# Attention and a SoLU feed-forward in one kernel: where the exponentials are added up, when a transpose is issued, and in which PSUM banks outputs lie

## The chip, the cores and the metric

The kernel runs on one core of a Trainium2 chip. The time is that of the device, in microseconds (us), as the median of several runs; lower is better. A profile of one execution shows every instruction of the core's engines: TensorE (PE, with its weight loads as PEld), VectorE (DVE), ScalarE (ACT), GpSimd (POOL) and SyncE (SP), which issues most of the transfers.

## The reference

Two blocks are joined. The first is attention with normalised queries and keys, for 8 batches of 12 heads with 448 tokens and 64 columns. Its result, as 3584 rows of 768, goes through a feed-forward with a softmax-weighted unit and a layer norm.

```python
def _attn_ref(q, k, v, g_q, g_k):                     # q, k, v: (8, 12, 448, 64) float32
    def rmsnorm(x, g):
        rms = np.sqrt(np.mean(x * x, axis=-1, keepdims=True) + 1e-06)
        return x / rms * g
    q_n, k_n = (rmsnorm(q, g_q), rmsnorm(k, g_k))
    scores = 1.0 / np.sqrt(q.shape[-1]) * np.matmul(q_n, k_n.transpose(0, 1, 3, 2))
    scores = scores - np.max(scores, axis=-1, keepdims=True)
    attn = np.exp(scores)
    attn = attn / (np.sum(attn, axis=-1, keepdims=True) + 1e-09)
    return np.matmul(attn, v)

def _moe_ref(x, w_in, w_out, g_ln):                   # x: (3584, 768), w_in: (768, 1024), w_out: (1024, 768)
    h = x @ w_in
    e = np.exp(h - np.max(h, axis=-1, keepdims=True))
    solu = h * (e / (np.sum(e, axis=-1, keepdims=True) + 1e-09))
    mu = np.mean(solu, axis=-1, keepdims=True)
    var = np.mean((solu - mu) ** 2, axis=-1, keepdims=True)
    return ((solu - mu) / np.sqrt(var + 1e-06) * g_ln) @ w_out

# reference: x = attn_out.transpose(0, 2, 1, 3).reshape(B * S, H * D); return _moe_ref(x, ...)
```

The weights arrive as 64-bit floats; the kernel converts them to 32 bits on the chip.

## The kernel before

The kernel takes two heads at a time, a "pair" (48 of them). `h0` is on partitions 0 to 63 and `h1` on 64 to 127 of the tiles that have the head's columns on the partitions. Scores are computed with the keys on the partitions, in four pieces `kc` of 112 keys, and their exponentials E are used as they are: the values are summed over keys by TensorE, the sum of the exponentials too, by a matmul with ones, and the division comes last. PSUM has eight banks of 512 float32 a partition: tile `h` takes two, the two buffers of tag "t" two banks each, the two buffers of tag "o" one each.

```python
    loads = ctx.enter_context(tc.tile_pool(name="loads", bufs=2))
    work = ctx.enter_context(tc.tile_pool(name="work", bufs=2))
    small = ctx.enter_context(tc.tile_pool(name="small", bufs=4))
    ps_h = ctx.enter_context(tc.tile_pool(name="ps_h", bufs=1, space=bass.MemoryType.PSUM))
    ps_t = ctx.enter_context(tc.tile_pool(name="ps_t", bufs=2, space=bass.MemoryType.PSUM))
    # ...
    def normalise(n):
        d = st[n]
        d["qkn"] = work.tile([P, 2 * NB, 32], FP32, tag="qkn", name="qkn", bufs=1)
        nc.gpsimd.tensor_tensor(
            d["qkn"],
            d["qk"].rearrange("p s b d -> p (s b) d"),
            d["y"].rearrange("p b -> p b ()").to_broadcast([P, 2 * NB, 32]),
            OP.mult,
        )

    def qk_transpose(n):
        d = st[n]
        d["qkT"] = work.tile([P, 2, S], FP32, tag="qkT", name="qkT")
        nc.vector.transpose(d["qkT"].rearrange("p s t -> p (s t)"), d["qkn"].rearrange("p b d -> p (b d)"))

    def gain(n):
        d = st[n]
        nc.scalar.activation(d["qkT"][:, 0], d["qkT"][:, 0], AF.Copy, scale=gcol[:, KF : KF + 1])

    def fold_sums(n):
        d = st[n]
        nc.vector.tensor_tensor(d["ss"], d["ss"], d["part"], OP.add)

    def scores(n, kc):
        d = st[n]
        if kc == 0:
            d["E"] = work.tile([SP, NJ, 2, S], FP32, tag="E", name="E")
        s = ps_t.tile([SP, 2, 512], FP32, tag="t", name="s")
        for h in range(2):
            hh = slice(h * D, (h + 1) * D)
            nc.tensor.matmul(
                s[:, h, 0:S], d["qkT"][hh, 1, kc * SP : (kc + 1) * SP], d["qkT"][hh, 0, :], start=True, stop=True
            )
        nc.scalar.activation(d["E"][:, kc], s[:, :, 0:S], AF.Exp)

    def add(n, kc):
        d = st[n]
        if kc == 1:
            d["es"] = work.tile([SP, 2, S], FP32, tag="es", name="es")
            nc.gpsimd.tensor_tensor(d["es"], d["E"][:, 0], d["E"][:, 1], OP.add)
        else:
            nc.vector.tensor_tensor(d["es"], d["es"], d["E"][:, kc], OP.add)

    def values(n):
        d = st[n]
        d["o"] = ps_t.tile([P, S], FP32, tag="o", name="o")
        for kc in range(NJ):
            for h in range(2):
                nc.tensor.matmul(
                    d["o"][h * D : (h + 1) * D, :], d["v"][:, h, kc], d["E"][:, kc, h],
                    start=(kc == 0), stop=(kc == NJ - 1),
                )

    def sums(n):
        d = st[n]
        d["sm"] = ps_t.tile([P, S], FP32, tag="o", name="sm")
        for h in range(2):
            nc.tensor.matmul(
                d["sm"][h * D : (h + 1) * D, :], ones[0:SP, :], d["es"][:, h], start=True, stop=True
            )

    def divide(n):
        b, hp = divmod(n, NP)
        d = st[n]
        if b // 2 not in xTs:
            xTs[b // 2] = work.tile([P, KD, 2 * S], FP32, tag="xT", name="xT")
        r = work.tile([P, NB, 32], FP32, tag="r", name="r", bufs=1)
        rc = small.tile([P, NB], FP32, tag="rc", name="rc")
        nc.vector.transpose(r.rearrange("p b i -> p (b i)"), d["sm"])
        nc.vector.reciprocal(rc, r[:, :, 0])
        nc.vector.transpose(r, rc.rearrange("p b -> p b ()").to_broadcast([P, NB, 32]))
        c0 = (b % 2) * S
        nc.vector.tensor_tensor(xTs[b // 2][:, hp, c0 : c0 + S], d["o"], r.rearrange("d b i -> d (b i)"), OP.mult)
        del st[n]
```

The feed-forward works on tiles of 128 rows: two halves of h, a softmax and a layer norm (`ff_max`, `ff_moments`, `ff_norm`, issued one, two and three units later), the transpose of u, and two halves of the output.

```python
    def ff_in(t, half):
        m, i = divmod(t, 2 * S // P)
        d = mt.setdefault(t, {})
        if half == 0:
            d["h"] = ps_h.tile([P, DFF], FP32, tag="h", name="h")
        hs = slice(half * 512, half * 512 + 512)
        for c in range(KD):
            nc.tensor.matmul(
                d["h"][:, hs], xTs[m][:, c, i * P : (i + 1) * P], w_in[:, c, hs], start=(c == 0), stop=(c == KD - 1)
            )
    # ... ff_max, ff_moments, ff_norm: VectorE, ScalarE and one power on GpSimd; u is 128x1024
    def ff_transpose(t):
        d = mt[t]
        d["uT"] = work.tile([P, KF, P], FP32, tag="uT", name="uT")
        pt = ps_t.tile([P, KF, P], FP32, tag="t", name="pu")
        for c in range(KF):
            nc.tensor.transpose(pt[:, c], d["u"][:, c * P : (c + 1) * P], ident)
        nc.scalar.copy(d["uT"][:, 0 : KF // 2], pt[:, 0 : KF // 2])
        nc.vector.tensor_copy(d["uT"][:, KF // 2 : KF], pt[:, KF // 2 : KF])

    def ff_out(t, half):
        d = mt[t]
        if half == 0:
            d["y"] = work.tile([P, DM], FP32, tag="y", name="y")
        hs = slice(half * HO, (half + 1) * HO)
        po = ps_t.tile([P, HO], FP32, tag="t", name="po")
        for c in range(KF):
            nc.tensor.matmul(po, d["uT"][:, c], w_out[:, c, hs], start=(c == 0), stop=(c == KF - 1))
        nc.scalar.copy(d["y"][:, hs], po)
        if half == 1:
            nc.scalar.dma_start(out[t * P : (t + 1) * P, :], d["y"])
            del mt[t]
```

A weight piece is converted in four steps, one at each call of `step()`: the low bits on ScalarE, the high bits on VectorE, their join on VectorE, and for w_out a product with the layer norm's gain on ScalarE. The pieces of w_in are spread over pairs 0 to 11, those of w_out over pairs 12 to 21.

```python
    # ... convert_w: the four steps
    wq = [(moe_w_in, w_in, c, slice(i * 512, i * 512 + 512)) for c in range(KD) for i in range(2)]
    n_in = len(wq)
    wq += [(moe_w_out, w_out, c, slice(i * HO, i * HO + HO)) for c in range(KF) for i in range(2)]
    W_IN = 12
    W_OUT = 22
    # ...
    def second(t, a, b):
        return [(W_OUT + 1, lambda: ff_transpose(t)), a, (W_OUT + 1, lambda: ff_out(t, 0)), b, (W_OUT + 1, lambda: ff_out(t, 1))]

    nothing = (0, None)
    for t in range(NT):
        ready = -(-(t + 1) * P // S) * NP + 1
        a = (max(ready, W_IN + 1), lambda t=t: ff_in(t, 0))
        b = (max(ready, W_IN + 1), lambda t=t: ff_in2(t))
        waiting.append(t)
        if len(waiting) > (LAG if t < NT - 8 else 1):
            c, _, d, _, e = second(waiting.pop(0), nothing, nothing)
            events += [a, c, b, d, e]
        else:
            events += [a, b]
    for t in waiting:
        events += [x for x in second(t, nothing, nothing) if x[1]]
```

The order of the instructions is fixed by hand in this loop (`unit` runs a piece of TensorE work and then what `later` has put down for that time):

```python
    N = B * NP
    # ... first loads, and the preparation of pairs 0 to 2
    with tc.manual_schedule():
        at = 0
        for n in range(N):
            due = []
            while at < len(events) and len(due) < (4 if n > W_OUT else 1) and events[at][0] <= n:
                due.append(events[at][1])
                at += 1
            def ff(k):
                for f in due[len(due) * k // 3 : len(due) * (k + 1) // 3]:
                    unit(f)
            unit(lambda: scores(n, 0))
            if n:
                add(n - 1, 3)
            if n + 2 < N:
                fold_sums(n + 2)
            unit(lambda: scores(n, 1))
            step()
            ff(0)
            if n:
                unit(lambda: values(n - 1))
            add(n, 1)
            if n + 1 < N:
                qk_transpose(n + 1)
            if n + 2 < N:
                rsqrt_seed(n + 2)
            if n + 3 < N:
                squares(n + 3)
            if n + 4 < N:
                load(n + 4)
            if n + 1 < N:
                gain(n + 1)
                load_v(n + 1)
            if n + 2 < N:
                rsqrt_step(n + 2)
                normalise(n + 2)
            if n + 3 < N:
                row_sums(n + 3)
            step()
            for _ in stages:
                load_next()
            if n:
                unit(lambda: sums(n - 1))
                later(1, lambda n=n: divide(n - 1))
            if n + 3 < N:
                swap_sums(n + 3)
            step()
            begin(n + 1)
            ff(1)
            unit(lambda: scores(n, 2))
            unit(lambda: scores(n, 3))
            add(n, 2)
            ff(2)
        add(N - 1, 3)
        unit(lambda: values(N - 1))
        unit(lambda: sums(N - 1))
        divide(N - 1)
        # ... the rest of the feed-forward, and the check of the weights

```

The rest is cut: the loads, the sums of squares and their inverse root (`squares`, `row_sums`, `swap_sums`; `rsqrt_seed` on ScalarE begins with a logarithm of the folded sums, `rsqrt_step` is three small VectorE instructions), the check of the weights' range, and a second, general path that is not taken for these inputs.

Of the kernel before, what the change touches and what calls it, by code (L numbers as in the profile page):

```python
# [9 lines left out]
FP32 = mybir.dt.float32  # L10
# [356 lines left out]
def fast_path(  # L367
# [20 lines left out]
    P = 128  # L388
# [7 lines left out]
    NT = B * S // P  # L396
    LAG = 4
# [202 lines left out]

    def add(n, kc):
        d = st[n]
        if kc == 1:
            d["es"] = work.tile([SP, 2, S], FP32, tag="es", name="es")
            nc.gpsimd.tensor_tensor(d["es"], d["E"][:, 0], d["E"][:, 1], OP.add)  # L605
        else:
            nc.vector.tensor_tensor(d["es"], d["es"], d["E"][:, kc], OP.add)  # L607
# [13 lines left out]
    def sums(n):  # L621
        d = st[n]
        d["sm"] = ps_t.tile([P, S], FP32, tag="o", name="sm")
        for h in range(2):
            nc.tensor.matmul(  # L625
                d["sm"][h * D : (h + 1) * D, :], ones[0:SP, :], d["es"][:, h], start=True, stop=True
            )
# [18 lines left out]
    mt = {}  # L646

# [41 lines left out]
    def ff_transpose(t):  # L689
        d = mt[t]  # L690
        d["uT"] = work.tile([P, KF, P], FP32, tag="uT", name="uT")
        pt = ps_t.tile([P, KF, P], FP32, tag="t", name="pu")
        for c in range(KF):
            nc.tensor.transpose(pt[:, c], d["u"][:, c * P : (c + 1) * P], ident)  # L694
        nc.scalar.copy(d["uT"][:, 0 : KF // 2], pt[:, 0 : KF // 2])  # L695
        nc.vector.tensor_copy(d["uT"][:, KF // 2 : KF], pt[:, KF // 2 : KF])  # L696

    def ff_out(t, half):
# [4 lines left out]
        po = ps_t.tile([P, HO], FP32, tag="t", name="po")  # L703
# [35 lines left out]
    W_IN = 12  # L739
    W_OUT = 22  # L740
# [20 lines left out]
    def step():  # L761
        for c in stages:
            c.pop(0)()
# [30 lines left out]
    with tc.manual_schedule():  # L794
# [17 lines left out]
        for n in range(N):  # L812
# [12 lines left out]
            if n:  # L825
                add(n - 1, 3)
            if n + 2 < N:
                fold_sums(n + 2)
            unit(lambda: scores(n, 1))
            step()  # L830
            ff(0)
# [3 lines left out]
            add(n, 1)  # L835
            if n + 1 < N:
                qk_transpose(n + 1)
# [6 lines left out]
            if n + 1 < N:  # L844
                gain(n + 1)
                load_v(n + 1)
# [8 lines left out]
            if n:  # L855
                unit(lambda: sums(n - 1))
                later(1, lambda n=n: divide(n - 1))
            if n + 3 < N:
                swap_sums(n + 3)
            step()  # L860
            begin(n + 1)
            ff(1)
# [3 lines left out]
            add(n, 2)  # L866
# [4 lines left out]
        divide(N - 1)  # L871

# [86 lines left out]
```

## Time and profile before

| | |
|---|---|
| time, median of three runs | 1117.56 us (1117.32 to 1121.18) |
| span of the profiled execution | 1116.4 us |
| mean clock granted to TensorE | 0.976 of full speed |
| instructions | 10449 |
| GpSimd additions of E (`es<-E`, 112x896) | 48, mean 2207 ns, 106.0 us busy |
| VectorE additions (`es<-es,E`, 112x896) | 96, mean 1176 ns, 112.9 us busy |
| sum matmuls (`sm<-es,ones`) | 192 passes, 45.3 us busy |
| VectorE transposes of q and k (`qkT<-qkn`) | 48, mean 1103 ns |
| ScalarE gains (`qkT<-qkT,gcol`) | wait 47.6 us in 29 cases for the transpose |

A float32 matmul of the program counts as two in the profile, one for each pass; the column "x" counts passes. Busy time is a share of the span, and a mean over stages that have different limits. A row of the timeline gives the start, the duration, the engine, the line of the kernel, the operation with the tiles that it writes and reads, and in brackets the idle time of the engine before it, with what ended that. A row of the waits says which instruction waited for which, for how long in total, how often, and how long at most.

### The profile page before, as it was taken

To read this page: it belongs to the slowest core of one execution; us is meant where nothing else is said; L and a number is where in the kernel's file an instruction comes from. 1 tells how busy PE (TensorE), PEld (TensorE's weight loads), DVE (VectorE), ACT (ScalarE), POOL (GpSimd) and SP (SyncE) were. 2 spreads that over 40 slices of the span, in tenths; PEclk is the share of its full clock that TensorE was granted. 3 is DMA by queue.
4 is the path that set the end of the run, shared out by engine and by line. 5 is a ranking of instruction groups with operands and counts; after the bars stand their busy time and mean duration, and the time that the engine had idled before them with its cause. 6 is when DMAs were issued, how large, how long until landed. Compare 5 with 4: busy or idle time off the path is not lost.

```text
span 1116.4 us, 10449 instructions
## 1 busy us (share of the span) xinstructions
PE 1002.6 (90%) x3523; PEld 445.3 (40%) x3523; DVE 651.1 (58%) x1013; ACT 383.9 (34%) x645; POOL 258.9 (23%) x326
## 2 busy tenths in 40 slices
PE   2868769878899989999999999999999999999997
PEld 0222223223334434444444444444444444455554
DVE  4999997987874355434455453545554344455521
ACT  4665656455452223223233232232332222111110
POOL 3544433432331121111222120311211111000000
PEclk8898989999999999999999999999999999999999
DMA  7554444423231111111111112212111002033330
GB/s 150 132 118 107 103 91 92 98 53 87 51 64 40 39 39 26 39 39 39 40 39 40 25 39 48 52 34 48 29 27 32 22 23 80 14 128 113 112 128 33
DMA packets 234425, 70.09 MB, mean 63 GB/s; under 512 B 223600, under 2 KB 223608, under 8 KB 234360
## 3 DMA queue, kind: packets, MB, share of 16 engines
q1 hardware_dynamic: 230016, 58.23, 23.7%
q10 hardware_dynamic: 4344, 11.08, 2.5%
q8 instruction: 30, 0.49, 0.2%
q14 instruction: 35, 0.29, 0.1%
HBM read 58.27 MB, written 11.01 MB: 62 GB/s over the span
## 4 chain that ended last, share of the span: by engine, by line
PE 69%; DVE 19%; ACT 7%; issue 2%; POOL 1%; DMA 0%; SPq 0%; ACTq 0%; DVEq 0%; POOLq 0%
PE po L705 27%; PE h L655 24%; PE o L616 9%; PE s L596 6%; DVE es L607 4%; ACT E L599 3%; PE pu L694 2%; PE sm L625 2%; DVE qkT L583 2%; DVE part L540 2%; DVE tmp L467 2%; DVE hmax L665 2%; DVE w_in L471 1%; ACT u L668 1%; DVE tmp L466 1%
## 5 line engine op out<-in xcount | busy, mean ns | idle before, releaser
L705 PE MATMUL po<-w_out,uT 128*128 128x384 f32 x896 | 301.1, 492 | 22.0 <-ACT E L599 19.9
L655 PE MATMUL h<-w_in,xT 128*128 128x512 f32 x672 | 302.5, 600 | 0.0
L596 PE MATMUL s<-qkT 64*112 64x448 f32 x768 | 188.5, 608 | 63.2 <-ACT E L599 32.6
L705 PEld LDWEIGHTS po<-w_out,uT 128*128 128x128 f32 x896 | 168.3, 191 | 156.9 <-ACT E L599 34.6
L599 ACT ACTIVATE E<-s 112x896 f32<-112x896 f32 x192 | 166.9, 912 | 96.9 <-PE s L596 96.9
L655 PEld LDWEIGHTS h<-w_in,xT 128*128 128x128 f32 x672 | 124.2, 191 | 164.5 <-issue 162.6
L616 PE MATMUL o<-E,v 112*64 112x448 f32 x768 | 160.1, 560 | 0.0
L605 POOL TENSOR_TENSOR es<-E 112x896 f32<-112x896 f32 x48 | 106.0, 2207 | 180.5 <-ACT E L599 162.1
L607 DVE TENSOR_TENSOR es<-es,E 112x896 f32<-112x896 f32 x96 | 112.9, 1176 | 59.4 <-ACT E L599 56.3
L683 POOL TENSOR_TENSOR he<-he,mhalf 128x1 f32<-128x1 f32 x28 | 21.8, 779 | 496.1 <-DVE he L682 496.1
L596 PEld LDWEIGHTS s<-qkT 64*112 64x112 f32 x768 | 62.4, 182 | 173.7 <-ACT E L599 74.4
L706 ACT COPY y<-po 128x384 f32<-128x384 f32 x56 | 26.8, 479 | 251.2 <-PE po L705 244.6
L696 DVE COPY uT<-pu 128x512 f32<-128x512 f32 x28 | 19.4, 692 | 156.0 <-ACT uT L695 156.0
L573 POOL TENSOR_TENSOR qkn<-qk,ny 128x896 f32<-128x896 f32 x48 | 81.4, 1696 | 101.0 <-DVE ny L568 79.8
L616 PEld LDWEIGHTS o<-E,v 112*64 112x64 f32 x768 | 52.4, 141 | 104.6 <-issue 86.2
L668 ACT ACTIVATE u<-h,hmax 128x1024 f32<-128x1024 f32 x28 | 31.2, 1113 | 156.9 <-DVE hmax L665 156.9
L665 DVE TENSOR_REDUCE hmax<-h 128x1 f32<-128x1024 f32 x28 | 34.3, 1224 | 86.5 <-PE h L655 86.5
L625 PE MATMUL sm<-es,ones 112*64 112x448 f32 x192 | 45.3, 550 | 15.5 <-DVE es L607 15.5
L566 DVE TENSOR_TENSOR nx<-nx,ny 128x28 f32<-128x28 f32 x48 | 28.7, 597 | 50.3 <-ACT ny L562 50.3
L540 DVE TENSOR_REDUCE part<-sq 128x28 f32<-128x896 f32 x48 | 51.8, 1080 | 4.8 <-ACT sq L535 4.8
L583 DVE STREAM_TRANSPOSE qkT<-qkn 128x896 f32<-128x896 f32 x48 | 52.9, 1103 | 1.9 <-POOL qkn L573 1.9
L549 POOL COPY ss<-part 32x28 f32<-32x28 f32 x192 | 49.2, 256 | 20.7 <-DVE part L540 11.8
(65 smaller groups left out, 634.4 us busy)
## 6 DMA issues: line engine op xcount, KB each, us to landing
raw<-in_moe_w_in_dram SPq DMA_DIRECT2D x24, 512.0 KB, 4.4
raw<-in_moe_w_out_dram SPq DMA_DIRECT2D x32, 384.0 KB, 3.4
qk<-in_q_dram SPq DMA_DIRECT2D x192, 56.0 KB, 2.1
qk<-in_k_dram SPq DMA_DIRECT2D x192, 56.0 KB, 2.2
v<-in_v_dram SPq DMA_DIRECT2D x48, 224.0 KB, 2.7
out_dram<-y ACTq DMA_DIRECT2D x28, 384.0 KB, 2.3
grow<-in_g_q_dram ACTq DMA_DIRECT2D x2, 0.2 KB
grow<-in_g_k_dram ACTq DMA_DIRECT2D x2, 0.2 KB
```

Source lines behind the costliest of these rows:

```text
L540: nc.vector.tensor_reduce(d["part"], d["sq"], AX, OP.add)
L573: nc.gpsimd.tensor_tensor(d["qkn"], d["qk"].rearrange("p s b d -> p (s b) d"), d["y"].rearrange("p b -> p b ()").to_broadcast([P, 2 * NB, ...
L583: nc.vector.transpose(d["qkT"].rearrange("p s t -> p (s t)"), d["qkn"].rearrange("p b d -> p (b d)"))
L596: nc.tensor.matmul(s[:, h, 0:S], d["qkT"][hh, 1, kc * SP : (kc + 1) * SP], d["qkT"][hh, 0, :], start=True, stop=True)
L599: nc.scalar.activation(d["E"][:, kc], s[:, :, 0:S], AF.Exp)
L605: nc.gpsimd.tensor_tensor(d["es"], d["E"][:, 0], d["E"][:, 1], OP.add)
L607: nc.vector.tensor_tensor(d["es"], d["es"], d["E"][:, kc], OP.add)
L616: nc.tensor.matmul(d["o"][h * D : (h + 1) * D, :], d["v"][:, h, kc], d["E"][:, kc, h], start=(kc == 0), stop=(kc == NJ - 1),)
L625: nc.tensor.matmul(d["sm"][h * D : (h + 1) * D, :], ones[0:SP, :], d["es"][:, h], start=True, stop=True)
L655: nc.tensor.matmul(d["h"][:, hs], xTs[m][:, c, i * P : (i + 1) * P], w_in[:, c, hs], start=(c == 0), stop=(c == KD - 1))
L665: nc.vector.tensor_reduce(nmax, d["h"], AX, OP.max, negate=True)
L705: nc.tensor.matmul(po, d["uT"][:, c], w_out[:, c, hs], start=(c == 0), stop=(c == KF - 1))
```

## The change

It has three parts. In pairs 0 to 11, beside the conversion of w_in, GpSimd no longer adds exponentials: VectorE adds E0 and E1 into one tile and E2 and E3 into another, and TensorE adds the two sums up by accumulating two matmuls with ones into the same bank. It is meant to keep GpSimd's additions away from VectorE in that stretch. In the later pairs the additions stay as they were. Second, VectorE transposes the next pair's q and k right after the pending addition, ahead of its other work for the pair, and ScalarE applies the gain later, after the conversion of the next weight pieces has begun. The load of the next values is issued later too. Third, the transposed u and the outputs of the feed-forward take the one-bank buffers of values and sums (tag "o") in the first and the last of a pair's three places for feed-forward pieces, and those of the scores (tag "t") in the middle place and after the last pair. In tag "o" the transposed u is two tiles of one bank instead of one tile of two. It is meant to free the outputs from the exponentials that read the scores' banks.

```diff
--- before.py
+++ after.py
@@ -394,6 +394,8 @@
     KF = DFF // P
     HO = DM // 2
     NT = B * S // P
+    W_IN = 12
+    W_OUT = 22
     LAG = 4
     assert H * D == DM and 2 * D == P and NJ * SP == S and S % 32 == 0 and B % 2 == 0 and 2 * S % P == 0
 
@@ -598,13 +600,21 @@
             )
         nc.scalar.activation(d["E"][:, kc], s[:, :, 0:S], AF.Exp)
 
     def add(n, kc):
         d = st[n]
-        if kc == 1:
-            d["es"] = work.tile([SP, 2, S], FP32, tag="es", name="es")
-            nc.gpsimd.tensor_tensor(d["es"], d["E"][:, 0], d["E"][:, 1], OP.add)
-        else:
-            nc.vector.tensor_tensor(d["es"], d["es"], d["E"][:, kc], OP.add)
+        two = n < W_IN
+        if kc in (1, 3) and two:
+            d["es", kc] = work.tile([SP, 2, S], FP32, tag="es", name="es")
+            nc.vector.tensor_tensor(d["es", kc], d["E"][:, kc - 1], d["E"][:, kc], OP.add)
+        elif kc == 1:
+            d["es", 3] = work.tile([SP, 2, S], FP32, tag="es", name="es")
+            nc.gpsimd.tensor_tensor(d["es", 3], d["E"][:, 0], d["E"][:, 1], OP.add)
+        elif not two:
+            nc.vector.tensor_tensor(d["es", 3], d["es", 3], d["E"][:, kc], OP.add)
 
     def values(n):
 
@@ -621,10 +631,13 @@
     def sums(n):
         d = st[n]
         d["sm"] = ps_t.tile([P, S], FP32, tag="o", name="sm")
-        for h in range(2):
-            nc.tensor.matmul(
-                d["sm"][h * D : (h + 1) * D, :], ones[0:SP, :], d["es"][:, h], start=True, stop=True
-            )
+        tiles = [d["es", kc] for kc in (1, 3) if ("es", kc) in d]
+        for i, es in enumerate(tiles):
+            for h in range(2):
+                nc.tensor.matmul(
+                    d["sm"][h * D : (h + 1) * D, :], ones[0:SP, :], es[:, h],
+                    start=(i == 0), stop=(i == len(tiles) - 1),
+                )
 
     def divide(n):
 
@@ -644,6 +657,7 @@
 
 
     mt = {}
+    ring = "t"
 
     def ff_in(t, half):
         m, i = divmod(t, 2 * S // P)
@@ -689,18 +703,23 @@
     def ff_transpose(t):
         d = mt[t]
         d["uT"] = work.tile([P, KF, P], FP32, tag="uT", name="uT")
-        pt = ps_t.tile([P, KF, P], FP32, tag="t", name="pu")
+        HK = KF // 2
+        if ring == "t":
+            pt = ps_t.tile([P, KF, P], FP32, tag="t", name="pu")
+            parts = [pt[:, 0:HK], pt[:, HK:KF]]
+        else:
+            parts = [ps_t.tile([P, HK, P], FP32, tag="o", name="pu") for _ in range(2)]
         for c in range(KF):
-            nc.tensor.transpose(pt[:, c], d["u"][:, c * P : (c + 1) * P], ident)
-        nc.scalar.copy(d["uT"][:, 0 : KF // 2], pt[:, 0 : KF // 2])
-        nc.vector.tensor_copy(d["uT"][:, KF // 2 : KF], pt[:, KF // 2 : KF])
+            nc.tensor.transpose(parts[c // HK][:, c % HK], d["u"][:, c * P : (c + 1) * P], ident)
+        nc.scalar.copy(d["uT"][:, 0:HK], parts[0])
+        nc.vector.tensor_copy(d["uT"][:, HK:KF], parts[1])
 
     def ff_out(t, half):
         d = mt[t]
         if half == 0:
             d["y"] = work.tile([P, DM], FP32, tag="y", name="y")
         hs = slice(half * HO, (half + 1) * HO)
-        po = ps_t.tile([P, HO], FP32, tag="t", name="po")
+        po = ps_t.tile([P, HO], FP32, tag=ring, name="po")
         for c in range(KF):
             nc.tensor.matmul(po, d["uT"][:, c], w_out[:, c, hs], start=(c == 0), stop=(c == KF - 1))
         nc.scalar.copy(d["y"][:, hs], po)
@@ -736,8 +755,6 @@
     wq = [(moe_w_in, w_in, c, slice(i * 512, i * 512 + 512)) for c in range(KD) for i in range(2)]
     n_in = len(wq)
     wq += [(moe_w_out, w_out, c, slice(i * HO, i * HO + HO)) for c in range(KF) for i in range(2)]
-    W_IN = 12
-    W_OUT = 22
     extent = consts.tile([P, 2, len(wq)], FP32, name="extent")
     raws = []
     stages = []
@@ -824,26 +841,25 @@
             unit(lambda: scores(n, 0))
             if n:
                 add(n - 1, 3)
+            if n + 1 < N:
+                qk_transpose(n + 1)
             if n + 2 < N:
                 fold_sums(n + 2)
             unit(lambda: scores(n, 1))
             step()
+            ring = "o"
             ff(0)
 
             if n:
                 unit(lambda: values(n - 1))
-            add(n, 1)
-            if n + 1 < N:
-                qk_transpose(n + 1)
+            if n >= W_IN:
+                add(n, 1)
             if n + 2 < N:
                 rsqrt_seed(n + 2)
             if n + 3 < N:
                 squares(n + 3)
             if n + 4 < N:
                 load(n + 4)
-            if n + 1 < N:
-                gain(n + 1)
-                load_v(n + 1)
             if n + 2 < N:
                 rsqrt_step(n + 2)
                 normalise(n + 2)
@@ -855,20 +871,27 @@
             if n:
                 unit(lambda: sums(n - 1))
                 later(1, lambda n=n: divide(n - 1))
+            if n + 1 < N:
+                load_v(n + 1)
             if n + 3 < N:
                 swap_sums(n + 3)
             step()
             begin(n + 1)
+            if n + 1 < N:
+                gain(n + 1)
+            ring = "t"
             ff(1)
 
             unit(lambda: scores(n, 2))
             unit(lambda: scores(n, 3))
-            add(n, 2)
+            add(n, 1 if n < W_IN else 2)
+            ring = "o"
             ff(2)
         add(N - 1, 3)
         unit(lambda: values(N - 1))
         unit(lambda: sums(N - 1))
         divide(N - 1)
+        ring = "t"
 
         last = events[at:]
         assert len(last) > len(wq) + 1
```

## The prediction

> **What bounds the kernel now.** I read the totals, then the busy time by stretches, because the 48 head pairs do not all carry the same work: pairs 0 to 11 run beside the conversion of w_in, 12 to 22 beside that of w_out with the first half of the feed-forward, and from pair 23 on the whole feed-forward is mixed in. The softmax divisions (line 637, one per pair) put the borders near 155 us and 335 us; after about 930 us little but feed-forward is left. First the totals, then four stretches (span; busy time and count of PE, PEld, DVE, ACT, POOL; clock; DMA share; GB/s).
>
> ```profile
> PE 1002.6 (90%) x3523; PEld 445.3 (40%) x3523; DVE 651.1 (58%) x1013; ACT 383.9 (34%) x645; POOL 258.9 (23%) x326
> ```
> ```profile
> 30.00:155.00 125.00, 95.38 (x416) 30.79 (x412) 121.25 (x166) 76.87 (x123) 61.13 (x69) 0.92 0.50 109
> 155.00:335.00 180.00, 152.35 (x549) 56.37 (x550) 149.62 (x238) 95.18 (x163) 62.89 (x76) 0.94 0.35 75
> 335.00:930.00 595.00, 569.13 (x1959) 261.11 (x1959) 289.87 (x445) 171.25 (x289) 117.29 (x147) 1.00 0.16 36
> 930.00:1116.40 186.40, 176.88 (x582) 93.66 (x582) 76.51 (x139) 26.82 (x46) 5.19 (x7) 0.99 0.28 91
> ```
>
> The "90% PE" is an average over unlike stages. In the first, VectorE is busy 121.25 of 125 us (97%) and TensorE 76%: VectorE is the bound. In the third TensorE is busy 96% and VectorE 49%. The second is mixed.
>
> Next, one pair of the first stage on VectorE in order of time (start, duration, engine, line, operation, count):
>
> ```profile
> 62.08 3.98 DVE L607 TENSOR_TENSOR es<-es,E 112x896 f32<-112x896 f32 x2
> 65.98 0.17 DVE L553 TENSOR_TENSOR ss<-ss,part 128x28 f32<-128x28 f32 x1
> ...
> 67.13 1.10 DVE L583 STREAM_TRANSPOSE qkT<-qkn 128x896 f32<-128x896 f32 x1
> ...
> 69.66 1.41 DVE L471 TENSOR_TENSOR w_in<-tmp 128x512 uint32<-128x512 uint32 x1
> ...
> 73.17 1.08 DVE L607 TENSOR_TENSOR es<-es,E 112x896 f32<-112x896 f32 x1
> ```
> ```profile
> 62.95 2.16 POOL L605 TENSOR_TENSOR es<-E 112x896 f32<-112x896 f32 x1 [2.17 <-ACT E L599]
> ```
> ```profile
> 41.71 2.07 DVE L553 TENSOR_TENSOR ss<-ss,part 128x28 f32<-128x28 f32 x1
> ```
>
> No row has an idle mark, so the pair lasts what VectorE needs: 62.08 to 73.17, 11.09 us. Two additions take 3.98 us, where a single one takes 1.08; GpSimd's addition runs from 62.95 to 65.11 and the second one ends after it. In the other example a 28-element addition that takes 0.17 us takes 2.07. One VectorE instruction in each pair is held while GpSimd adds.
>
> Last, what TensorE waited for in the third stage (total us, times, longest):
>
> ```profile
> PE po L705 <- ACT E L599: 18.0, 18, 2.2
> PE s L596 <- DVE uT L696: 5.5, 10, 1.4
> PE pu L694 <- ACT E L599: 2.4, 9, 0.3
> ```
>
> These are all of its waits there, 25.9 us of 595. An output matmul does not use E: what it waits for is its PSUM buffer, which an exponential is still reading. Scores, the transposed u and the outputs share the two buffers of tag "t".
>
> **What the Trainium skill says.** "SBUF — State Buffer", section "Who interferes with whom": VectorE with two SBUF inputs and a GpSimd instruction that reads SBUF use one shared read interface, and whoever comes second waits for the whole instruction of the other. The trace agrees (0.17 to 2.07 us, 1.08 to about 2.8), and its stream transpose, with one input, stays at 1.10. "Perfetto Trace Analysis", section "Optimization Strategy": the same gap repeating on the engine that should be saturated can mean too few buffers for the next tile; the 18 like waits above are that. "TensorE: Matmul & The Clock Gate", section "What's actually happening": the clock halves after idle windows and comes back under load. The trace has clock 0.92 in the stage where TensorE idles and 1.00 in the third, so a fuller TensorE should not be clocked lower.
>
> **Part 1: no GpSimd additions in pairs 0 to 11.** Removed: twelve of the 48 GpSimd additions, 2.1 to 2.9 us each, on an engine that bounds nothing. VectorE still does two additions a pair (E0+E1, E2+E3 instead of two accumulations), so its own work does not change. What goes is the holding. For each of the twelve I took the VectorE instruction that overlaps it and subtracted the usual duration of that row: 0.90, 0.92, 1.89, 1.89, 1.71, 1.71, 1.89, 1.78, 1.70, 1.70, 1.88, 1.77, together 19.7 us. As VectorE is without idle time there, all would come off the end if nothing else took over. A pair goes to 11.09 - 1.71 = 9.4 us. The product q·1/rms stays on GpSimd and goes on holding the 1.41 us join (L471).
>
> Added: two sum matmuls a pair. Two take 0.92 us (x4 passes) alone; in a run with others I estimate 0.8, from the values' 3.23 us for 16 passes. TensorE at full clock then has 2 x 1.76 (scores) + 3.23 (values) + 0.92 + 0.8 = 8.5 us per pair: below 9.4, but 0.9 us below instead of some 2.5. ScalarE's instructions sum to about 7.2 us. So VectorE stays the bound, except where a stretch at half clock lands in a pair (a clock of 0.92 is some 20 of the 125 us at half, 0.08 x 125 / 0.5): the record has such stretches of 3.4 us, and one costs up to 1.7 us against 0.9 of slack. I take 2 us off for that: **-18 us**.
>
> **Part 2: transpose first, gain later.** The order of instructions shows VectorE's transpose moved ahead of the sum of squares' fold, and ScalarE's gain behind the conversion of the low weight bits. Nothing is added. In the first stage ScalarE's 0.49 us wait for the transpose goes, off the bound. In the second it cuts both ways. Where GpSimd's remaining addition holds the 1024-element normalise (2.57 instead of 0.82 us, in every second pair), the 1.1 us transpose now runs inside that hold: up to 0.9 us each, five times, -4.5. But ScalarE there waits 2 to 3 us for the join (L471) before it can scale w_out, and the gain (0.67 us) used to fit into that wait; now it stands behind it, and the next exponentials, for which scores and VectorE's third addition already wait, come 0.6 us later, in some six pairs: +3.5. Net **-1 us**.
>
> **Part 3: outputs and transposed u in the banks of tag "o"** when they come before the values or after the scores, that is in two of the three places of a pair. The TensorE order is otherwise the same, so this only changes whose release is waited for. At these places the last users of "o" are the values and sums of an earlier pair, and their reader, the division, ended well before: in one pair it ended at 591.5 us, and the output matmuls that waited 1.67 us for an exponential started at 597.9. The 18.0 us should nearly all go, most of the 2.4 too; of the 5.5 about half stays, since transposes in the middle place keep tag "t". New: values right after a transpose of u need its first bank, and ScalarE copies that (0.6 us) only after the second exponential; about 0.6 us in one pair in five, five times, 3 us. 18.0 + 2.0 + 2.7 - 3.0 = 19.7; with the one like wait of the second stage (1.7) and some lost to waits not seen here: **-19 us**.
>
> Sum: 1117.6 - 18 - 1 - 19 = 1079.6, rounded to **1080 us**.
>
> **The rivals.** (a) *TensorE becomes the bound of the first stage.* For: only 0.9 us of slack, and those 20 us at half clock. Against: half clock follows idleness, and idleness shrinks. If it happens the stage gives 10 instead of 18 us: 1088. (b) *The new banks bring as many waits as they remove.* The values and sums stand behind ScalarE's and VectorE's copies, which are in queues behind other work. For: two banks of "o" for four users. Against: the places were chosen so that divisions are long over. If all is given back: 1098. (c) *The late gain and the late fold delay the exponentials everywhere*, also in the third stage, where ScalarE's logarithm now waits 1.1 us longer for the fold and holds what is queued behind it. For: ScalarE already waits for that fold 42.8 us in the first 280 us. Against: between the second and third exponentials of a pair TensorE has values, sums and mostly a feed-forward piece, 4 to 9 us. Cost if so: up to 10 us, 1090. (d) *The second stage gains more*, VectorE no longer being held at the worst places: 1072.
>
> **Range and chances.** The first part rests on durations and a saturated engine, the third on waits named one by one; that both fail is unlikely. One failing gives 1088 to 1098, so the range is 1068 to 1097. Faster by 2% means below 1095: 0.85; within 2%: 0.13; slower: 0.02.
>
> **What would show it.** Right: divisions of the first stage 9.3 to 9.7 us apart; no VectorE addition there above 1.2 us; TensorE busy near 90% in it; no output matmul waiting for E in the third stage and its idle time below 10 us; values sometimes waiting for ScalarE's uT. Wrong: scores of the first stage waiting with VectorE idle as well; idle time of the third stage moved to o or sm instead of gone; the second stage longer than 180 us.

## The result, and the profile after

The changed kernel takes 1072.34 us (median of four runs, 1071.4 to 1073.19) against 1118.42 us: a ratio of 0.9584, with a 95% interval of 0.9564 to 0.9605. The span of the profiled execution went from 1116.4 to 1069.6 us. I cut both by the divisions on VectorE, one in each pair (us):

| stretch | before | after | difference |
|---|---|---|---|
| start to the division of pair 0 | 37.3 | 35.4 | -1.9 |
| divisions of pairs 0 to 11 (w_in converted) | 122.5 | 103.2 | -19.3 |
| divisions of pairs 11 to 22 (w_out converted) | 162.4 | 165.4 | +3.0 |
| divisions of pairs 22 to 45 (whole feed-forward) | 611.6 | 584.0 | -27.6 |
| the rest | 182.5 | 181.5 | -1.0 |

The start lasts from 35 to 40 us in the later runs too, whatever was changed in them, so its 1.9 us are not put down to the change.

Busy time by stretches of the kernel after, with borders that stand where those of before stood (span; PE, PEld, DVE, ACT, POOL with counts; clock; DMA share; GB/s):

```profile
30.00:134.00 104.00, 94.22 (x464) 32.61 (x464) 100.77 (x170) 75.77 (x127) 31.27 (x55) 1.00 0.64 132
134.00:316.00 182.00, 156.24 (x555) 57.81 (x552) 151.43 (x234) 94.25 (x161) 64.41 (x77) 0.92 0.35 74
316.00:884.00 568.00, 562.63 (x1951) 259.33 (x1949) 280.97 (x445) 168.54 (x288) 119.04 (x146) 1.00 0.17 37
884.00:1069.60 185.60, 176.69 (x583) 93.77 (x582) 77.39 (x139) 26.71 (x46) 7.09 (x8) 1.00 0.28 91
```

In the first stretch VectorE is still busy 97% of the time, now over 104 instead of 125 us; TensorE stands at 91% and its clock at 1.00 instead of 0.92. In the third TensorE went from 96 to 99%.

One pair of the first stage on VectorE, kernel after:

```profile
74.61 2.08 DVE L612 TENSOR_TENSOR es<-E 112x896 f32<-112x896 f32 x2
76.61 1.10 DVE L585 STREAM_TRANSPOSE qkT<-qkn 128x896 f32<-128x896 f32 x1
77.64 0.14 DVE L555 TENSOR_TENSOR ss<-ss,part 128x28 f32<-128x28 f32 x1
...
80.45 1.31 DVE L473 TENSOR_TENSOR w_in<-tmp 128x512 uint32<-128x512 uint32 x1
...
83.86 1.08 DVE L612 TENSOR_TENSOR es<-E 112x896 f32<-112x896 f32 x1
```

Two additions take 2.08 us (3.98 before), and the pair 74.61 to 83.86, 9.25 us, again without an idle mark. The third stage's waits of TensorE:

```profile
PE s L598 <- DVE uT L715: 2.3, 5, 0.5
PE o L626 <- ACT uT L714: 2.1, 4, 0.5
PE pu L713 <- ACT uT L714: 1.0, 1, 1.0
```

No output matmul (`po`) waits any more; 5.4 us are left of 25.9. The two lines with ACT are new.

### The profile page after: what moved, and what is told of

It reads as the page before. It is cut to its first block, busy times and chain, and to the rows that moved or that the text cites. A ratio compares the mean times of both kernels' runs of the same rounds, so it can differ in the third digit from the quotient of the medians.

```text
span 1069.6 us, 10556 instructions
## 1 busy us (share of the span) xinstructions
PE 998.1 (93%) x3571; PEld 446.4 (42%) x3571; DVE 623.6 (58%) x1013; ACT 379.3 (35%) x645; POOL 232.1 (22%) x314
## 4 chain that ended last, share of the span: by engine, by line
PE 69%; DVE 17%; ACT 7%; issue 3%; SPq 1%; DMA 0%; POOL 0%; ACTq 0%; DVEq 0%
PE po L724 28%; PE h L669 23%; PE o L626 7%; PE s L598 7%; DVE part L542 2%; DVE qkT L585 2%; PE sm L637 2%; PE pu L713 2%; DVE es L612 2%; ACT E L601 1%; DVE es L617 1%; DVE tmp L473 1%; DVE tmp L469 1%; DVE w_in L473 1%; DVE ss L555 1%
## 5 line engine op out<-in xcount | busy, mean ns | idle before, releaser
L598 PE MATMUL s<-qkT 64*112 64x448 f32 x768 | 181.2, 590 | 44.0 <-ACT E L601 29.6
L626 PE MATMUL o<-E,v 112*64 112x448 f32 x768 | 156.3, 549 | 2.6 <-ACT uT L714 2.6
L617 DVE TENSOR_TENSOR es<-es,E 112x896 f32<-112x896 f32 x72 | 80.2, 1114 | 57.5 <-ACT E L601 55.6
L615 POOL TENSOR_TENSOR es<-E 112x896 f32<-112x896 f32 x36 | 76.6, 2128 | 143.5 <-ACT E L601 129.7
L715 DVE COPY uT<-pu 128x512 f32<-128x512 f32 x28 | 19.3, 690 | 149.5 <-ACT uT L714 86.9
L637 PE MATMUL sm<-es,ones 112*64 112x448 f32 x240 | 56.1, 564 | 11.4 <-DVE es L617 10.2
L687 DVE TENSOR_TENSOR u<-h,u 128x1024 f32<-128x1024 f32 x28 | 34.3, 1224 | 31.5 <-ACT u L682 31.3
```

The source lines that it names most:

```text
L598: nc.tensor.matmul(s[:, h, 0:S], d["qkT"][hh, 1, kc * SP : (kc + 1) * SP], d["qkT"][hh, 0, :], start=True, stop=True)
L615: nc.gpsimd.tensor_tensor(d["es", 3], d["E"][:, 0], d["E"][:, 1], OP.add)
L617: nc.vector.tensor_tensor(d["es", 3], d["es", 3], d["E"][:, kc], OP.add)
L626: nc.tensor.matmul(d["o"][h * D : (h + 1) * D, :], d["v"][:, h, kc], d["E"][:, kc, h], start=(kc == 0), stop=(kc == NJ - 1),)
L637: nc.tensor.matmul(d["sm"][h * D : (h + 1) * D, :], ones[0:SP, :], es[:, h], start=(i == 0), stop=(i == len(tiles) - 1),)
```

## The experiments

**Each part alone.** First the three parts of the change, each put into the kernel before. The first, with `add` and `sums` as in the diff of the change, and in the loop:

```diff
-            add(n, 1)
+            if n >= W_IN:
+                add(n, 1)
...
-            add(n, 2)
+            add(n, 1 if n < W_IN else 2)
```

> The kernel before with the first part alone: no GpSimd additions in pairs 0 to 11, two tiles of sums added up by TensorE; order and banks as before. If the hold of VectorE by GpSimd is what the first stage loses, the divisions of pairs 0 to 11 come 9.3 us apart instead of 11.1 and the run takes 1097 to 1099 us (19 to 21 us less), with all else as before. If the earlier transpose is needed too, because ScalarE's gain still waits for it, the distance stays at 9.8 us or more and the run takes 1103 us or more.

Measured: 1099.29 us, ratio 0.9811 (0.9788 to 0.9835). The divisions of pairs 0 to 11 are 9.2 to 9.3 us apart (the last distance 10.5), and the stretch takes 103.0 us, the same as with all three parts; the second and third stage are as before (162.8 and 610.3 us). So the hold explains the first stage, and the earlier transpose is not needed for it.

The third part, only the banks, with `ff_transpose` and `ff_out` as in the diff of the change, and in the loop:

```diff
+            ring = "o"
             ff(0)
...
+            ring = "t"
             ff(1)
...
+            ring = "o"
             ff(2)
```

> The kernel before with the third part alone: outputs and transposed u in the banks of tag o at the first and last place of a pair. If the banks alone account for the third stage, the stretch between the divisions of pairs 22 and 45 falls from 612 to 584 us, TensorE's idle time in it from 27.5 to 5 or 6 us, and the run takes 1090 to 1093 us. If the new order of transpose and gain had a share in the stage, it stays at 590 us or more and the run takes 1097 us or more.

Measured: 1097.58 us, 0.9791 (0.9769 to 0.9813); the third stage 589.3 us, its idle time 9.3 us. That is 22.3 of the 27.6 us, and the prediction for the banks alone failed: the order has a share. Of the waits of TensorE in the third stage one line shows which:

```profile
PE po L711 <- DVE r L637: 4.0, 4, 1.0
```

The output waits here for the division (`r`) to let go of the "o" banks. With the transpose moved ahead, VectorE reaches the division earlier, and the line is gone from the kernel after. One such division with the banks alone, then the same one in the kernel after:

```profile
564.41 0.64 DVE L637 STREAM_TRANSPOSE r<-sm 128x448 f32<-128x448 f32 x1
```
```profile
537.67 0.64 DVE L650 STREAM_TRANSPOSE r<-sm 128x448 f32<-128x448 f32 x1
```

The scores just ahead of the output start at 562.35 us in the first and at 537.84 us in the second: the division comes 2.1 us after them in the one and 0.2 us before them in the other.

The second part, only the order (transpose to the front, gain and load of values back, as in the diff above):

> The kernel before with the second part alone: transpose first, gain and the load of values later. My theory now: it costs 3 to 4 us in the second stage, where the fold of the sums lands in GpSimd's addition, and gives nothing elsewhere, so 1117 to 1123 us. The rival, that it gives what the sum of the other two parts lacks: 1112 us or less. In the first stage one VectorE instruction in each pair is still held for 1.7 to 1.9 us, only another one, and the distance of the divisions stays at 11.0 to 11.3 us.

Measured: 1113.03 us, 0.9928 (0.9905 to 0.9951). I was wrong on the first stage: the divisions come 10.3 us apart, not 11.1, and it takes 115.1 us. A VectorE and a GpSimd timeline of one pair show why:

```profile
87.08 1.10 DVE L583 STREAM_TRANSPOSE qkT<-qkn 128x896 f32<-128x896 f32 x1
88.11 1.05 DVE L553 TENSOR_TENSOR ss<-ss,part 128x28 f32<-128x28 f32 x1
```
```profile
86.16 2.96 POOL L605 TENSOR_TENSOR es<-E 112x896 f32<-112x896 f32 x1 [2.57 <-DMA qk<-in_k_dram]
```

The addition on GpSimd ends at 89.12 us. The transpose, with one input, runs beside it unhindered (1.10 us); only what is left of the addition then holds the fold, 0.9 instead of 1.7 to 1.9 us. What a GpSimd addition costs depends on what VectorE runs beside it. The second stage is 164.4 us (+2.0), the third 610.0, as before. The three parts alone give -20.8, -22.5 and -7.0 us, together -50.3; the change gives -46.1. In the first stage the first two parts take away the same hold (19.5 and 7.4 us alone, 19.3 with all three); in the third the second and the last help each other (1.6 and 22.3 us alone, 27.6 together).

**Is it the hold, or VectorE's own work?** The changed kernel, with one addition of each pair back on GpSimd:

```diff
-            nc.vector.tensor_tensor(d["es", kc], d["E"][:, kc - 1], d["E"][:, kc], OP.add)
+            (nc.gpsimd if kc == 1 else nc.vector).tensor_tensor(d["es", kc], d["E"][:, kc - 1], d["E"][:, kc], OP.add)
...
-            if n >= W_IN:
-                add(n, 1)
+            add(n, 1)
...
-            add(n, 1 if n < W_IN else 2)
+            if n >= W_IN:
+                add(n, 2)
```

> The changed kernel, but in pairs 0 to 11 GpSimd adds E0 and E1 into the first of the two tiles; VectorE adds E2 and E3 alone. VectorE so has one addition less in each pair (1.08 us), and GpSimd's addition is back. If the hold is the cost, a pair goes from 9.25 to 9.25 - 1.0 + 1.75, about 10.0 us, and the run is about 8 us slower than the changed kernel (1080). If it was not the hold but the number of VectorE's instructions or TensorE that sets the pace, a pair takes 8.3 to 9.3 us and the run is as fast or up to 9 us faster (1063 to 1072).

Measured: 1065.61 us (1065.02 to 1067.44), 0.9512 (0.9489 to 0.9535), so faster than the change; a pair takes mostly 8.4 to 8.8 us. The numbers are those of the rival. But the same instructions in pairs 0 to 11 stand in the next kernel, which has them in pairs 12 to 21 too (`two = n < W_OUT`):

> As the run with GpSimd adding E0 and E1 into a tile of their own, now in pairs 0 to 21: VectorE has one addition less in the second stage too (11 x 1.08 us), TensorE two matmuls more (11 x 0.8 us), and GpSimd's addition can hold VectorE. If what a GpSimd addition costs depends on what VectorE runs beside it, the place behind the release of the sums' tile keeps most of the hold away, and the stretch between the divisions of pairs 11 and 22 falls from 164.5 to 152 to 158 us, the run to 1053 to 1060 us. If the hold stays at 1.6 us a pair, the stretch stays above 160 us.

Measured: 1079.93 us, 0.9612 (0.9565 to 0.966), its four times 1079.87, 1079.99, 1070.02 and 1080.36. In the profile its first stage goes at 10.1 us a pair, the pace that the hold theory had named, and the second stage takes 167.3 us. One pair of each on VectorE, GpSimd and TensorE; first the faster pace:

```profile
79.47 0.19 DVE L570 SCALAR_TENSOR_TENSOR ny<-nx,ny 128x28 f32<-128x28 f32 x1
79.72 1.09 DVE L542 TENSOR_REDUCE part<-sq 128x28 f32<-128x896 f32 x1
```
```profile
79.58 2.10 POOL L612 TENSOR_TENSOR es<-E 112x896 f32<-112x896 f32 x1 [2.31 <-DMA qk<-in_k_dram]
```
```profile
78.48 1.67 PE L637 MATMUL sm<-es,ones 112*64 112x448 f32 x8
```

Then the slower pace:

```profile
113.10 2.08 DVE L568 TENSOR_TENSOR nx<-nx,ny 128x28 f32<-128x28 f32 x1
```
```profile
112.63 2.50 POOL L612 TENSOR_TENSOR es<-E 112x896 f32<-112x896 f32 x1 [3.99 <-ACT nx L563]
```
```profile
111.53 1.67 PE L637 MATMUL sm<-es,ones 112*64 112x448 f32 x8
```

In both the addition starts 1.10 us after the sums (79.58 - 78.48, 112.63 - 111.53), and it does so in every pair of the stage from the fourth on. So it most likely waits for its tile, which the sums of the pair before have to read first, though the brackets name other engines. In the first it comes as the last small two-input instruction ends, and falls beside the reduction; in the second it comes 0.5 us before the first of them and holds it for 1.9 us. Where TensorE is behind, the addition comes late and does not disturb; where VectorE is held, TensorE is ahead and the addition comes early. So both count, the hold and VectorE's own work: at the slower pace the hold takes more than the addition that VectorE was spared (10.1 us a pair against 9.25), at the faster it does not. That each pace keeps itself up in this way is argued from the two profiles, and neither pace holds throughout: the faster profile has one pair of 10.4 us, and the slower ends its first stage with two of 9.0 and 8.3 us, in which the addition (134.41 and 142.84 us) falls beside the reduction again. That the one time of 1070.02 us ran at the faster pace is likely, but it has no profile.

The second stage of this run (167.3 us) warns against a rule made of holds alone. GpSimd's additions hold VectorE there for 9.0 us in all, against 17.8 in the changed kernel, and VectorE has an addition less in each pair, and still the stage is not shorter.

**Choosing the place.** If the place decides, it can be chosen. The addition goes behind the swap of the sums on GpSimd (first in pairs 0 to 11, then in pairs 0 to 21 with the early gain):

```diff
-            add(n, 1)
...
                 swap_sums(n + 3)
+            if n < W_IN:                  # n < W_OUT in the second run
+                add(n, 1)
```

> As the run in which GpSimd adds E0 and E1 into a tile of their own in pairs 0 to 11, but the addition is issued on GpSimd behind the normalised q and k and the swap of the sums, not ahead of them. If what an addition on GpSimd costs depends on VectorE's instruction beside it, it now falls beside the division's transposes and reciprocal, which have one input, in every execution: no VectorE instruction but the join is held, a pair takes 8.4 to 8.6 us (TensorE's own 8.5), and the four times agree within 3 us at 1063 to 1068. If the two paces of 8.5 and 10.1 us have another cause than the place, both show up again.

> The same in pairs 0 to 21, with the gain in its old place. First stage as in the run before this one (8.4 to 8.6 us a pair). Second stage: VectorE has 11 additions less than with no GpSimd addition at all (11.9 us), so if VectorE sets it, the stretch between the divisions of pairs 11 and 22 falls below 150 us and the run takes 1046 to 1055 us; if TensorE, with its two more sums a pair, or ScalarE's chain sets it, it stays at 153 to 158 us and the run takes 1055 to 1062 us.

Measured: 1071.67 us (1070.7 to 1072.07), 0.9564 (0.9548 to 0.958), and 1059.31 us (1058.43 to 1060.35), 0.9459 (0.9443 to 0.9474). One pace only, as said, but 8.9 us a pair in both, not 8.4 to 8.6; the second stage of the latter takes 154.2 us. (The first's whole time shows little of its 3.7 us in the first stage: the start took 39.0 us in its profile.) The addition, from 93.70 to 95.79 us, still reaches VectorE's next one (in the second of the two runs):

```profile
94.92 1.82 DVE L612 TENSOR_TENSOR es<-E 112x896 f32<-112x896 f32 x1
```

So it went ahead of the swap:

```diff
+            if n < W_OUT:
+                add(n, 1)
             if n + 3 < N:
                 swap_sums(n + 3)
-            if n < W_OUT:
-                add(n, 1)
```

> As the run before, but GpSimd adds between the normalised q and k and the swap of the sums, 0.8 us earlier. In the run before each pair of the first stage loses about 0.7 us because the addition (93.70 to 95.79 us in one pair) still runs when VectorE begins to add E2 and E3 (94.92 us, held to 96.74). If it is this overlap alone, it goes away and a pair takes 8.4 to 8.5 us instead of 8.92, TensorE's own work; the first stage is 4 to 5 us shorter and the run takes 1053 to 1056 us. If the addition, following the normalisation at once, holds the join of VectorE for its whole length instead (VectorE waits already, but GpSimd does not let go between its two instructions), a pair takes 9.9 us or more and the run 1068 us or more.

Measured: 1056.44 us (1055.67 to 1057.78), ratio 0.9432 (0.9419 to 0.9445): the fastest version here. A pair of the first stage takes 8.3 to 8.5 us, and all holds of VectorE by that addition in the stage sum to 0.4 us. VectorE and GpSimd:

```profile
94.30 1.31 DVE L473 TENSOR_TENSOR w_in<-tmp 128x512 uint32<-128x512 uint32 x1
...
97.16 0.62 DVE L654 TENSOR_TENSOR xT<-o,r 128x448 f32<-128x448 f32 x1
97.89 1.12 DVE L612 TENSOR_TENSOR es<-E 112x896 f32<-112x896 f32 x1
```
```profile
93.37 1.70 POOL L575 TENSOR_TENSOR qkn<-qk,ny 128x896 f32<-128x896 f32 x1 [2.28 <-issue]
95.03 2.52 POOL L612 TENSOR_TENSOR es<-E 112x896 f32<-112x896 f32 x1
```

The addition ends at 97.55 us, before VectorE's own begins. TensorE is now the bound of the first stage: 2.9 us idle in it. The second stage takes 159.5 us, 5 more than with the later place: in four of its pairs the addition holds the second of two joins, and the two take 3.6 us together where the later place has 1.75. The two places were not combined.

**The second stage.** Why +3.0 us? The figure itself is loose. From pair 12 to pair 22 the kernel before has the same instructions as the runs with the first and the third part alone (but for the banks in the last pair), and the stretch takes 162.4, 162.8 and 164.4 us in them. The changed kernel has the same there as the run with the order alone and the two that put an addition back on GpSimd in pairs 0 to 11 only: 165.4, 164.4, 164.5 and 165.7 us. By the means (163.2 and 165.0) the change costs about 2 us there, and a difference of 1 or 2 us between two single profiles says little. Two edits of the changed kernel: the fold ahead of the transpose, and the gain back in its old place.

```diff
+            if n + 2 < N:
+                fold_sums(n + 2)
             if n + 1 < N:
                 qk_transpose(n + 1)
-            if n + 2 < N:
-                fold_sums(n + 2)
```

> The changed kernel with one exchange on VectorE: the fold of the sums of squares (0.17 us) before the transpose instead of behind it. If the loss of 3 us in the second stage comes from the fold landing in GpSimd's addition (1.8 us instead of 0.15, and ScalarE's logarithm behind it), the stretch between the divisions of pairs 11 and 22 falls from 165.4 to 161 to 163 us, and the last two pairs of it from 10 to about 8.5 us each; the first stage stays at 9.25 us a pair. If it comes from the late gain, the stretch stays at 165 us.

Measured: 1072.82 us, 0.9581 (0.9565 to 0.9597); the second stage 162.3 instead of 165.4 us. The whole time does not show it; in this profile the start took 2.5 us longer than in that of the changed kernel.

```diff
+            if n + 1 < N:
+                gain(n + 1)
             if n + 2 < N:
                 rsqrt_step(n + 2)
...
             begin(n + 1)
-            if n + 1 < N:
-                gain(n + 1)
```

> The changed kernel with ScalarE's gain back in its old place, before the conversion of the low bits. If the late gain costs the second stage 0.6 us in some six pairs, as I predicted, the stretch between the divisions of pairs 11 and 22 falls from 165.4 to about 162 us; first stage and third stage as in the changed kernel. If the fold is the cause instead, it stays at 165 us.

Measured: 1070.39 us, 0.955 (0.9534 to 0.9566); the second stage 161.4 us. Both lie below all four values of the changed order, so both have a share, as far as one profile of each can show; they were not undone together. For the fold, VectorE of the changed kernel in this stage and the addition on GpSimd beside it:

```profile
289.52 1.77 DVE L555 TENSOR_TENSOR ss<-ss,part 128x28 f32<-128x28 f32 x1
291.94 0.19 DVE L568 TENSOR_TENSOR nx<-nx,ny 128x28 f32<-128x28 f32 x1 [0.64 <-ACT ny L564]
```
```profile
289.17 2.09 POOL L615 TENSOR_TENSOR es<-E 112x896 f32<-112x896 f32 x1 [4.46 <-ACT E L601]
```

In the kernel before, at the same point, the fold (310.30) is through before the addition (310.47) begins:

```profile
310.30 0.18 DVE L553 TENSOR_TENSOR ss<-ss,part 128x28 f32<-128x28 f32 x1
310.40 1.10 DVE L583 STREAM_TRANSPOSE qkT<-qkn 128x896 f32<-128x896 f32 x1
```

The fold behind the transpose is held, ScalarE's logarithm waits for the fold, and VectorE then waits for ScalarE. Before, the same addition held the small instruction behind the transpose instead, for 1.0 us (1.19 instead of 0.15).

In every second pair the addition meets the 1024-element normalise of the feed-forward. Pair 17 on VectorE, before, where the addition runs from 231.92 to 234.00 us:

```profile
231.99 2.57 DVE L687 TENSOR_SCALAR u<-u,mv,he 128x1024 f32<-128x1024 f32 x1 [0.35 <-POOL he L683]
```

And after, where it runs from 211.24 to 213.31 us:

```profile
211.80 1.55 DVE L555 TENSOR_TENSOR ss<-ss,part 128x28 f32<-128x28 f32 x1
213.28 0.80 DVE L701 TENSOR_SCALAR u<-u,mv,he 128x1024 f32<-128x1024 f32 x1
```

The transpose runs inside the addition, as foretold, and the normalise is free, but the fold behind the transpose takes over most of the hold: 1.41 instead of 1.75 us. The normalise also shows that one input does not always keep an instruction free: it reads one large tile, and was held.

Last, the first part of the change stretched to pairs 0 to 21 (`two = n < W_OUT`, and no GpSimd addition before it), and that with the early gain:

> The changed kernel with its first part stretched to pairs 0 to 21: GpSimd adds no exponentials there, TensorE adds two tiles of sums. The profile of the changed kernel shows 17.8 us of VectorE held by eleven additions in the second stage. If VectorE's time sets that stage, the stretch between the divisions of pairs 11 and 22 falls by 10 to 17 us, to 149 to 155 us, and the run takes 1057 to 1063 us. If TensorE (0.8 us more in each pair) or ScalarE's chain sets it, the stretch falls by less than 5 us.

> The changed kernel with no GpSimd additions in pairs 0 to 21 and the gain back in its old place. Taken alone these shortened the second stage by 7.6 and 4.0 us (165.4 to 157.8 and 161.4). If they take away different waits (VectorE's hold; ScalarE's queue), the stretch between the divisions of pairs 11 and 22 is 153 to 155 us and the run 4 us faster than with the first alone; if both shorten the same chain, it stays at 157 us.

Measured: 1067.59 us, 0.9531 (0.9515 to 0.9547), with a second stage of 157.8 us; and 1063.01 us, 0.9489 (0.9473 to 0.9504), with 157.1 us. The first lies between my two cases: of some 16 us of hold that went (17.8 to 1.7), 7.6 came off the stage. Part of that can be TensorE's clock, which rose in the stretch from 0.92 to 0.98. The early gain, worth 4.0 us alone, is worth 0.7 on top in these two profiles, as if both shortened one chain. But the profile of the first kernel belongs to the fastest of its four times (1063.43 us, the others 1067.33 to 1067.86), and by the medians the early gain is worth 4.6 us, what I had named for two different waits. So this stays open, and so does how the rest of the stage divides among VectorE, ScalarE's queue and TensorE.

## Why the prediction was right, point by point

- **Part 1**, -18 us: the stage gave 19.3, and with this part alone 19.5 (122.5 to 103.0). The holds were the cost, but the sum of twelve (19.7 us) fits in part by chance: two of them, 0.90 and 0.92 us, lie before the division of pair 0, and the ten inside the stretch make 17.9. The 2 us taken off for a half clock did not come: the clock rose to 1.00. Rival (a) is out; TensorE had more slack before than the "some 2.5" us of the prediction (11.1 less 7.7 is 3.4), and it became the bound only when VectorE had lost an addition more, at 8.4 us a pair, where I had worked out 8.5.
- **Part 2**, -1 us: this part was wrong, in the sign too. The second stage cost 3.0 us in the one pair of profiles and about 2 by all of them, and it went above the 180 us that I had named as a sign of being wrong (182.0 between the same borders). The cost of the late gain was about right (3.5 foretold, 4.0 measured by undoing it). The step that failed is the gain of 4.5 us from a transpose inside a hold. The normalise was freed in four pairs, but the fold, pushed behind the transpose, was held in its place for 1.41 of the 1.75 us: 0.34 us gained in a pair where I had up to 0.9. In all, these additions hold VectorE for 17.8 us in the stage, against 15.8 before, and moving the fold back gave 3.1 us. I had followed the transpose to its new place and not what it pushed back.
- **Part 3**, -19 us: the mechanism held, the size was off: 27.6. The 18.0 us of waits for E went entirely; 5.5 became 2.3; the new waits of the values for ScalarE's copy, 3.0 foretold, are 2.1. Idle time fell by 22.1 us (27.5 to 5.4), more than my sum of 19.7 less a reserve. The other 5.5 us are not in the idle time at all. Some 1.7 of them are a stretch at half clock in the kernel before (0.94 between 392 and 420 us). In one repetition of five pairs, 131.5 us before and 126.6 after, idle time gives 4.3 of the 4.9 us with 8 waits before and 2 after: each wait that went was worth about 0.1 us more than its idle time. Two groups of matmuls that follow without a wait overlap by 0.07 us in the record (kernel after: scores end at 564.36, outputs start at 564.29), and a wait loses that too. With some 27 waits fewer in the stage (37 to 10) this is an estimated 2.7 us; about 1 us is left without a cause.
- **Rivals.** (b) failed for the banks as changed, but was not empty: with the old order the outputs wait 4.0 us for the division. I had seen that the divisions ended "well before" from one pair; four pairs were otherwise. (c) held in the second stage alone. (d) is out, though its number, 1072, is the one that was measured: the second stage lost.
- **The sum**: 1080 foretold, 1072.3 measured, inside the range. In the span the change gave 8.8 us more than the 38 that I had: 8.6 more in the third stage, 1.3 in the first, 1.9 in the start and 1.0 in the rest, less 4.0 in the second. That the total came so near is partly luck, since the part that failed takes back nearly half of what the third stage gave beyond my sum.

## What to carry to other kernels

A GpSimd instruction costs VectorE what it overlaps of work that it can hold, not what it lasts: before moving it away, look for a place beside transposes, reductions and operands in PSUM, and away from additions, joins and a large scaling such as the normalise. Here, with all else alike, the additions kept on GpSimd in a good place gave 1056.4 us where their removal from pairs 0 to 21 gave 1063.0. All of that came from the first stage, where VectorE had been the bound and now had an addition less in each pair (101.4 to 92.0 us); in the second the same place cost 2.4 us (157.1 to 159.5). When an instruction is moved ahead in a queue, follow what it pushes back, and check a buffer's release in every pair of the pattern, not in one.

## What the runs showed of the hardware

- VectorE's transposes (1.10 us), reductions (1.09) and reciprocals (0.24) run beside a GpSimd addition unhindered, and so does a product with one input in PSUM. `xT<-o,r` takes 0.62 us alone, and 0.62 where the addition runs from 93.70 to 95.79 us beside it:

```profile
94.38 0.62 DVE L654 TENSOR_TENSOR xT<-o,r 128x448 f32<-128x448 f32 x1
```

- TENSOR_SCALAR instructions with one large input are held as two-input ones are: the normalise took 2.57 us instead of 0.82, and `tmp<-raw` 2.25 instead of 0.35 (kernel before, pair 16). The Trainium skill, "SBUF — State Buffer", section "Who interferes with whom", frees an instruction with at most one input in SBUF unless it runs in a two-port mode, which `tensor_scalar` can enter. The traces agree with the first half; of the second they show the hold and not the mode.
- The hold goes both ways, and is handed over between two instructions of GpSimd that follow at once: in the fastest run the join waits for the normalisation, gets its turn at the end of it (95.07 us) and ends at 95.61, and the addition behind it takes 2.52 instead of 2.09 us.
- One and the same order of instructions can settle into two paces, 8.4 to 8.8 and 10.1 us a pair; the two differ in when the addition on GpSimd starts against VectorE's instructions.
